# An attention and soft-mixture kernel on one core: EPS as a 33rd score column, wider products for phi and for three batches' slot averages, buffers given by a table, and the attention steps in another order

## The chip, the cores and the metric

The kernel runs on one core of a Trainium2 chip. The metric is the device time of one execution in microseconds (us), as the median of several runs. Lower is better.

## What is computed

Two stages, all in float32. Attention works on 8 batches of 8 heads, with 512 tokens and 32 state slots of 64 values each, in both directions:

```
scores = x @ state.T / 8;  a  = exp(scores - rowmax);  a  /= a.sum(-1) + 1e-09;  xread = a  @ state
scores2 = state @ x.T / 8; a2 = exp(scores2 - rowmax); a2 /= a2.sum(-1) + 1e-09; sread = a2 @ x
x = concatenate([xread, sread], axis=2), as 4608 rows of 512
```

Then a soft mixture of 8 experts with 4 slots each:

```
logits = x @ phi                                   # phi is 512 x 32
d = softmax(logits, axis 0);  slot_input = d.T @ x # 32 slots of 512
slot_out[e] = relu(slot_input[e] @ w1[e]) @ w2[e]  # w1[e] 512 x 1024, w2[e] 1024 x 512
out = softmax(logits, axis 1) @ slot_out
```

The softmaxes add EPS = 1e-09 to their sums. The weights w1 and w2 are 33.5 MB, x is 8.4 MB, and the result is 8.9 MB.

## The kernel before

**Transfers.** SyncE (SP) issues nearly all DMAs in one order: x and state first (L87 to L103), then 62 weight tiles of 512 KB and 4 of 256 KB (L112 for w2, L122 for w1), then the outputs (L789, L805). A tile pool "big" has 43 buffers of 4 KB per partition. The x tiles and the first 25 weight tiles fill it at the start. Each later weight load goes into a buffer that the kernel has finished with: two loads stand behind each batch's R step (its last use of x), one behind the later of S.7 and U.1, four 256 KB pieces go into attention's own buffers (step `load_half`), two into the "an" buffers (`load_an`), and the rest follow the w1 products, which free their weights. The framework gives each DMA one of eight semaphores in turn, and a DMA waits until the one eight places earlier has landed.

**Attention, about the first 77 us.** The order of its steps is written out by hand in the string ORDER: `X.2.1` is step X for batch 2 and head pair 1, `m2.3.0` step m2 for batch 3 and head parity 0. Engines run their own part of this list in order. The steps that matter here, for each batch b and half h:

- X, xe: TensorE (PE) turns x by 128x128 transposes; ScalarE (ACT) copies them out, scaled by 1/8 (L241). Two of batch 0 are on VectorE (DVE).
- S: scores, eight products with 32 stationary columns and 512 moving ones (L250).
- q, m1, sub, x1, l1, r1, mul, aT: token softmax. DVE turns 32x32 blocks (L263), DVE takes the maximum (L268), GpSimd (POOL) subtracts (L272), ACT takes exp (L275), DVE sums 32 scores (L279) into a two-column buffer l1s whose second column holds EPS, DVE sums those two columns (L283) and takes the reciprocal (L284), POOL multiplies (L288), DVE turns back (L293).
- m2, e2, l2: slot softmax. ACT writes its sums into l2s, again with an EPS column; DVE adds the two (L310) and inverts (L311).
- E, ee, A, ae: more PE transposes and their ACT copies (L326, L335).
- R, sr, srT, srTe: slot averages. R has 16 products per half, each with 32 stationary columns and 64 moving ones, for four groups g of 32 rows (L343). DVE scales them (L356), PE turns them (L361), ACT copies (L367).
- G, Ge: once, phi times all states: 32 products with 64 moving columns against a block-diagonal copy of phi (L206), copied by ACT (L215).
- For each pair of batches: Lx (logits), mx, mk, bm, nme (a running maximum), dx, dT, dTe, T, tt, Px, Y, which add the pair's part of slot_input into y. Ls to Ys do the same for the state rows.

The list ends with a serial stretch: the last Lx, mx.3, mk.3, bm.3, nme.3, dx.3, dT.3, dTe.3, T.3, tt.3, Px.3, Y.3, SI, SIe. SIe writes si_m, which the experts need.

**Experts and output, from about 77 us.** PE multiplies si_m by w1 (L680), turns the hidden rows (L701), and multiplies by w2 (L744), first for the left 256 columns (c = 0), then for the right. Output products (L778, L796) stand between the w2 products of c = 1; ACT and DVE copy them out (L787, L788), and SP sends them (L789).

Each kind of buffer is a rotating pool: 11 of tag "h" (2 KB), two "an", and the eight PSUM banks as 2 "sc", 3 "tr" and 3 "ms".

Of the kernel before, what the change touches and what calls it, by code (L numbers as in the profile page):

```python
# [28 lines left out]
ORDER = """
X.0.0 xe.0.0 X.0.1 xe.0.1 X.0.2 xe.0.2 X.0.3 xe.0.3 S.0 q.0.0 X.1.1 xe.1.1 X.1.2 xe.1.2 X.1.3 m2.0.0 e2.0.0  # L30
X.1.0 E.0.0 xe.1.3 m1.0.0 G.0 q.0.1 sub.0.0 m1.0.1 xe.1.0 m2.0.1 x1.0.0 l1.0.0 sub.0.1 r1.0.0 e2.0.1 l2.0 x1.0.1
X.2.1 xe.2.1 l1.0.1 Ge.0 S.1 ee.0.0 E.0.1 r1.0.1 ee.0.1 X.2.3 xe.2.3 R.0.0 q.1.0 m2.1.0 X.2.0 X.2.2 R.0.1 e2.1.0
mul.0.1 E.1.0 m2.1.1 m1.1.0 mul.0.0 q.1.1 xe.2.0 xe.2.2 e2.1.1 aT.0.1 X.3.2 sub.1.0 x1.1.0 X.3.3 aT.0.0 xe.3.3
S.2 xe.3.2 sr.0 X.3.1 m1.1.1 ee.1.0 xe.3.1 E.1.1 l1.1.0 m2.2.0 sub.1.1 x1.1.1 ee.1.1 X.3.0 q.2.0 srT.0 A.0.0
srTe.0 m2.2.1 R.1.0 q.2.1 Lx.0.0 ae.0.0 xe.3.0 R.1.1 e2.2.0 m1.2.0 l1.1.1 e2.2.1 Lx.0.1 r1.1.0 A.0.1 ae.0.1 l2.1
X.4.3 xe.4.3 m1.2.1 sr.1 r1.1.1 E.2.0 S.3 E.2.1 sub.2.0 x1.2.0 l2.2 mul.1.0 aT.1.0 q.3.1 ee.2.0 srT.1 m2.3.0
X.4.1 ee.2.1 mul.1.1 aT.1.1 X.4.0 X.4.2 Lx.1.0 m1.3.1 l1.2.0 R.2.0 Lx.1.1 xe.4.1 mx.0 srTe.1 R.2.1 A.1.0 xe.4.0
e2.3.0 m2.3.1 sub.2.1 x1.2.1 q.3.0 xe.4.2 mk.0 sr.2 l1.2.1 e2.3.1 E.3.0 ee.3.0 sub.3.1 A.1.1 ae.1.1 keep.0 bm.0
srT.2 r1.2.0 mul.2.0 S.4 nme.0 m1.3.0 R.3.0 X.5.3 dx.0 r1.2.1 mul.2.1 x1.3.1 q.4.0 l1.3.1 E.3.1 ae.1.0 xe.5.3
aT.2.0 X.5.1 aT.2.1 ee.3.1 dT.0 m1.4.0 X.5.0 m2.4.0 xe.5.1 A.2.0 dTe.0 sub.3.0 x1.3.0 srTe.2 l2.3 xe.5.0 e2.4.0  # L40
m2.4.1 q.4.1 sub.4.0 X.5.2 T.0 r1.3.1 R.3.1 Lx.2.0 m1.4.1 U.0 l1.3.0 ae.2.0 xe.5.2 tt.0 X.6.3 sr.3 mul.3.1
e2.4.1 x1.4.0 Ue.0 E.4.0 S.5 r1.3.0 A.2.1 srT.3 l1.4.0 ee.4.0 q.5.0 E.4.1 xe.6.3 sub.4.1 ae.2.1 X.6.1 x1.4.1
mul.3.0 X.6.2 Lx.2.1 R.4.0 l2.4 srTe.3 Ls.0 ee.4.1 r1.4.0 R.4.1 m2.5.1 aT.3.1 e2.5.1 Lse.0 aT.3.0 Lx.3.0 A.3.0
al.0 xe.6.2 xe.6.1 E.5.1 m2.5.0 e2.5.0 m1.5.0 sub.5.0 l1.4.1 ae.3.0 q.5.1 X.6.0 sr.4 xe.6.0 r1.4.1 mul.4.1
ee.5.1 Lr.0 msx.0 x1.5.0 Lx.3.1 Px.0 S.6 als.0 mx.1 mk.1 m1.5.1 dsx.0 lkp.0 E.5.0 A.3.1 l1.5.0 ee.5.0 sub.5.1
X.7.2 m2.6.1 R.5.0 Y.0 aT.4.1 m2.6.0 q.6.0 pv.1 X.7.3 bm.1 nme.1 ae.3.1 xe.7.2 mul.4.0 aT.4.0 X.7.0 m1.6.0
e2.6.1 r1.5.0 E.6.1 xe.7.3 e2.6.0 xe.7.0 l2.6 X.7.1 xe.7.1 R.5.1 srT.4 x1.5.1 V.0 q.6.1 l2.5 dx.1 Lu.0 m1.6.1
E.6.0 ee.6.0 sr.5 keep.1 D.0 l1.5.1 srTe.4 sub.6.1 S.7 pv.2 ee.6.1 q.7.1 mul.5.0 m2.7.1 srT.5 Ve.0 srTe.5 R.6.0
r1.5.1 mul.5.1 m2.7.0 Lx.4.0 q.7.0 R.6.1 aT.5.0 dT.1 dTe.1 Lx.4.1 A.4.1 sr.6 e2.7.1 T.1 tt.1 sub.6.0 A.4.0
e2.7.0 E.7.0 ae.4.1 x1.6.0 ee.7.0 Lus.0 m1.7.0 al.1 srT.6 E.7.1 sub.7.0 Lx.5.0 Ps.0 srTe.6 m1.7.1 aT.5.1 l1.6.0  # L50
A.5.1 sub.7.1 Ys.0 l2.7 Lu.1 r1.6.0 x1.6.1 l1.6.1 R.7.0 Lx.5.1 mx.2 mul.6.0 ee.7.1 R.7.1 sr.7 srT.7 ae.5.1
x1.7.0 r1.6.1 l1.7.0 ae.4.0 mk.2 mul.6.1 bm.2 nme.2 A.5.0 keep.2 srTe.7 Px.1 Ls.1 aT.6.0 x1.7.1 dx.2 ae.5.0 U.1
r1.7.0 mul.7.0 Lse.1 l1.7.1 dT.2 r1.7.1 mul.7.1 A.6.0 dTe.2 aT.6.1 al.2 Lx.6.0 aT.7.0 Y.1 Lr.1 msx.1 pv.3 dsx.1
lkp.1 Ue.1 Lx.6.1 Lx.7.0 T.2 ae.6.0 als.1 aT.7.1 Lx.7.1 mx.3 mk.3 A.6.1 ae.6.1 A.7.0 ae.7.0 bm.3 nme.3 dx.3 tt.2
A.7.1 Px.2 D.1 Y.2 dT.3 ae.7.1 dTe.3 V.1 Lu.2 al.3 windows keep.3 Ve.1 Lus.1 Lu.3 T.3 tt.3 Ps.1 Ys.1 load_half
load_an Wd We Px.3 spin.3 Y.3 SI SIe
"""
# [820 lines left out]
```

## Time and profile before

| what | us |
|---|---|
| median of 3 runs | 132.95 |
| lowest and highest run | 132.51, 133.6 |
| the profiled execution, whole | 132.75 |
| its span, first to last instruction | 130.9 |
| PE, DVE, ACT, POOL busy in the span | 116.0, 88.3, 76.8, 45.2 |

The profiled execution takes 1.85 us outside its span. Busy times are unions of an engine's instructions; matmuls are pipelined, so that PE's busy share overstates its load. The DMA share is the mean busy share of the core's 16 DMA engines, which can read slightly over 1.

### The profile page before, as it was taken

What the parts mean: (1) busy time and instruction counts of PE and PEld (TensorE: products, weight loads), DVE (VectorE), ACT (ScalarE), POOL (GpSimd) and SP (SyncE); (2) the same over time, 40 slices, a digit from 0 to 9 for tenths busy, and PEclk for the clock granted to TensorE, in tenths of its full rate; (3) what the DMA queues carried; (4) which work ended last, traced back from release to release, by engine and by line L of the source; (5) the groups of instructions that cost most, each with busy time, mean ns of one, the idle gap of its engine ahead of it and who ended that gap; (6) DMA issues with size and microseconds to landing.
All of it is one profiled execution on the core that took longest, in us unless ns stands there. A gap on an engine that the chain in (4) does not pass through costs nothing.

```text
span 130.9 us, 4551 instructions
## 1 busy us (share of the span) xinstructions
PE 116.0 (89%) x1854; PEld 76.2 (58%) x1854; DVE 88.3 (67%) x224; ACT 76.8 (59%) x187; POOL 45.2 (35%) x65
## 2 busy tenths in 40 slices
...
DMA  4999999999999999999999999999999999999991
GB/s 105 369 402 350 418 414 423 410 418 412 412 419 414 419 417 418 418 417 414 418 414 420 412 415 404 417 420 414 418 420 414 412 400 415 418 380 420 414 409 76
DMA packets 14852, 51.73 MB, mean 395 GB/s; under 512 B 1648, under 2 KB 1776, under 8 KB 14832
## 3 DMA queue, kind: packets, MB, share of 16 engines
...
q8 instruction: 14, 0.23, 0.6%
...
HBM read 42.53 MB, written 8.91 MB: 393 GB/s over the span
## 4 chain that ended last, share of the span: by engine, by line
DMA 57%; PE 31%; DVE 1%; issue 1%; ACT 1%; SPq 1%; DVEq 0%
DMA w<-w_in 45%; DMA x<-x_in 12%; PE so_ps L744 11%; PE h_ps L680 11%; PE o L778 6%; DVE out L788 1%; PE hT_ps L701 1%; PE sum_ps L764 1%; PE os L796 1%; ACT out L787 0%; SPq L89 0%; SPq L87 0%; PE si_ps L628 0%; ACT so_r L768 0%; DVE si_m L646 0%
## 5 line engine op out<-in xcount | busy, mean ns | idle before, releaser
L272 POOL TENSOR_TENSOR q<-q,m 128x512 f32<-128x512 f32 x16 | 16.7, 1048 | 15.4 <-DVE m L268 8.1
L241 ACT ACTIVATE xt<-xt_ps 128x512 f32<-128x512 f32 x30 | 17.9, 618 | 6.7 <-PE xt_ps L235 6.6
L288 POOL TENSOR_TENSOR q<-q,r 128x512 f32<-128x512 f32 x16 | 16.7, 1048 | 8.3 <-DVE r L284 2.7
L235 PE MATMUL xt_ps<-ident,x 128*128 128x128 f32 x112 | 16.0, 277 | 0.0
L744 PE MATMUL so_ps<-w,h_m 128*32 128x256 f32 x256 | 15.2, 381 | 0.0
L788 DVE COPY out<-o 128x512 f32<-128x512 f32 x16 | 10.3, 686 | 7.1 <-PE o L778 7.1
L680 PE MATMUL h_ps<-w,si_m 128*32 128x512 f32 x128 | 14.4, 594 | 0.4 <-DVE si_m L646 0.4
L787 ACT COPY out<-o 128x512 f32<-128x512 f32 x16 | 8.6, 590 | 8.9 <-PE o L778 8.9
L235 PEld LDWEIGHTS xt_ps<-ident,x 128*128 128x128 f32 x112 | 12.4, 141 | 2.3 <-issue 0.8
L744 PEld LDWEIGHTS so_ps<-w,h_m 128*32 128x32 f32 x256 | 7.7, 110 | 8.2 <-issue 2.3
L263 DVE STREAM_TRANSPOSE q<-sc 128x512 f32<-128x512 f32 x16 | 11.1, 695 | 1.1 <-PE sc L250 1.1
L304 ACT ACTIVATE e<-sc,nm 128x512 f32<-128x512 f32 x16 | 11.2, 706 | 0.6 <-DVE q L263 0.4
L680 PEld LDWEIGHTS h_ps<-w,si_m 128*32 128x32 f32 x128 | 9.1, 110 | 4.2 <-issue 2.3
L778 PE MATMUL o<-lt_all,so_r 32*128 32x512 f32 x64 | 10.7, 633 | 0.3
L293 DVE STREAM_TRANSPOSE aT<-q 128x512 f32<-128x512 f32 x16 | 10.8, 689 | 0.0
L279 DVE TENSOR_REDUCE l1s<-q 128x16 f32<-128x512 f32 x16 | 10.5, 656 | 0.0
L318 PE MATMUL eT_ps<-ident,e 128*128 128x128 f32 x64 | 9.9, 278 | 0.7 <-ACT e L304 0.5
L275 ACT ACTIVATE q<-q 128x512 f32<-128x512 f32 x16 | 10.5, 657 | 0.0
L268 DVE TENSOR_REDUCE m<-q 128x16 f32<-128x512 f32 x16 | 10.5, 659 | 0.0
L299 DVE TENSOR_REDUCE nm<-sc 128x1 f32<-128x512 f32 x16 | 10.5, 660 | 0.0
L318 PE MATMUL an_ps<-ident,aT 128*128 128x128 f32 x64 | 10.0, 280 | 0.2 <-DVE aT L293 0.2
L326 ACT COPY eT<-eT_ps 128x512 f32<-128x512 f32 x16 | 9.5, 608 | 0.3 <-PE eT_ps L318 0.3
...
## 6 DMA issues: line engine op xcount, KB each, us to landing
w<-w_in SPq DMA_DIRECT2D x62, 512.0 KB, 10.0
out_x<-out SPq DMA_DIRECT2D x16, 512.0 KB, 6.1
x<-x_in SPq DMA_DIRECT2D x14, 512.0 KB, 9.8
...
x_b<-x_in ACTq DMA_DIRECT2D x1, 512.0 KB, 4.6
...
```

What stands on the lines that cost most here:

```text
L235: pe.transpose(p[:, P * j : P * j + P], xg[b, g][:, j, :], ident)
L241: scaled(r[f"xt{g}"], r[f"xp{g}"], 0.125)
L263: dve.transpose(r[f"q{h}"], r[f"sp{h}"])
L272: pool.tensor_tensor(v, v, R[b][f"m1{h}"].broadcast_to([P, 16, NS]), op=ALU.subtract)
L288: pool.tensor_tensor(v, v, R[b][f"r1{h}"].broadcast_to([P, 16, NS]), op=ALU.mult)
L293: dve.transpose(r[f"aT{h}"], r[f"q{h}"])
L304: act.activation(r[f"e2{h}"], r[f"sp{h}"], AF.Exp, bias=r[f"nm2{h}"], accum_out=l2s[:, b % 2, h, 0:1])
L318: pe.transpose(p[:, j, :], r[f"{src}{h}"][:, P * j : P * j + P], ident)
L680: pe.matmul(h_ps[hf][32 * kt : 32 * kt + 32, :], si_m[kt // 2][:, 256 * (kt % 2) + 32 * e : 256 * (kt % 2) + 32 * e + 32], w1t[hf, e, kt], ...
L744: pe.matmul(so[c][32 * i : 32 * i + 32, :], h_m[hf][:, 256 * i + 32 * e : 256 * i + 32 * e + 32], w2t[c, e, 4 * hf + i], start=(hf == 0 an ...
L778: pe.matmul(o[j], so_r[hf][rows, col : col + 128], lt_all[rows, 4 * q : 4 * q + 4, :].rearrange("p b s -> p (b s)"), start=True, stop=True,)
L788: dve.tensor_copy(ot[:, 1, :], o[2 * jp + 1])
```

## The change

- The score tile q gets 33 columns for each token instead of 32. POOL writes EPS into the 33rd before `sub`, and `l1` sums 33 columns, so that L283 goes. The steps q, m1, sub, x1, mul and aT now walk over rows of 32 with a step of 33.
- e2 puts its sums straight into the tile l2; POOL adds EPS (new step `l2p`), and L310 goes.
- G takes phi itself as moving or stationary operand: 8 products with 256 moving columns and a contraction of 64 instead of 32 products with 64; Ge becomes two DVE transposes instead of an ACT copy, and the block-diagonal phi goes.
- R for batches 2, 4 and 6 (WIDE): per half 8 products with 64 stationary columns and 128 moving ones instead of 16 with 32 and 64. Half of what they write isn't used. sr is twice as wide there, and srT is two transposes.
- HOMES says by a letter which buffer each tile gets. DVE_STEPS names the copies that DVE makes instead of ACT. ORDER is a new list.
- SP's list of DMAs stays the same, in the same order; `load_half` stands earlier among the steps and `load_an` later.

The diff, cut to its core (line numbers of the new file differ):

```
 ORDER = """
-X.0.0 xe.0.0 X.0.1 xe.0.1 X.0.2 xe.0.2 X.0.3 xe.0.3 S.0 q.0.0 X.1.1 xe.1.1 X.1.2 xe.1.2 X.1.3 m2.0.0 e2.0.0
...
+X.0.0 X.0.2 xe.0.0 X.0.1 xe.0.2 X.0.3 xe.0.1 xe.0.3 X.1.1 S.0 xe.1.1 X.1.0 m2.0.1 X.1.3 xe.1.0 X.1.2 q.0.1
...
+COPIES = {"h": NH, "an": AN, "sc": 2, "tr": 3, "ms": 3}
+HOMES = {
...
+    "an": "abababbaab",
+    "sc": "abbaabababababab",
...
+DVE_STEPS = "Ve.1 ae.6.0 ae.7.1 dTe.3 lkp.1 mk.1 mk.3 xe.0.1 xe.1.1 xe.2.0"
+WIDE = (2, 4, 6,)
...
-    l1s = cp.tile([P, 4, 16, 2], F32, name="l1s")
-    l2s = cp.tile([P, 2, 2, 2], F32, name="l2s")
-    pool.memset(l1s, EPS)
-    pool.memset(l2s, EPS)
+    eps = cp.tile([P, 2, 1], F32, name="eps")
+    pool.memset(eps, EPS)
...
+        pools = {"h": wk, "an": wk, "sc": ps_s, "tr": ps_t, "ms": ps_m}
+        sizes = {"h": 16 * (NS + 1), "an": F, "sc": S, "tr": S, "ms": S}
+        def home(kind, shape, name):
+            k, n, table = made[kind], COPIES[kind], HOMES.get(kind)
+            made[kind] += 1
+            if table:
+                letter = table[k] if k < len(table) else chr(97 + (k - len(table)) % n)
+                t = pools[kind].tile([P, sizes[kind]], F32, tag=kind + letter, name=name, bufs=1)
...
+        def move(step, out, in_, scale=None):
+            if scale is None:
+                (dve.tensor_copy if step in on_dve else act.copy)(out, in_)
+            else:
+                (dve.tensor_scalar_mul if step in on_dve else act.mul)(out, in_, scale)
...
         def G(b):
-            for b in range(B):
-                for g in range(4):
+            for g in range(4):
+                for h in range(2):
+                    rows = slice(64 * h, 64 * h + 64)
                     pe.matmul(
-                        p[32 * g : 32 * g + 32, b, :],
-                        st_t(b, g),
-                        phi_bd[:, g].rearrange("p h n -> p (h n)"),
+                        gp[h][32 * g : 32 * g + 32].rearrange("p (q i) n -> p q i n", i=2),
+                        phi_sb[rows, g, :],
+                        stT_sb[rows, :, g % 2, g // 2, :, :],
...
         def Ge(b):
-            act.copy(G_sb, R[0]["gp"].rearrange("p b (h n) -> p b h n", h=2))
+            for h in range(2):
+                dve.transpose(G_sb[:, :, h, :], R[0]["gp"][h])
...
         def q(b, h):
-            r[f"q{h}"] = half(f"q{b}_{h}")
-            dve.transpose(r[f"q{h}"], r[f"sp{h}"])
+            t = home("h", [P, 16, NS + 1], f"q{b}_{h}")
+            r[f"qv{h}"] = t[:, :, 0:NS]
+            dve.transpose(r[f"qv{h}"], r[f"sp{h}"].rearrange("p (k n) -> p k n", n=NS))
...
         def sub(b, h):
+            pool.memset(R[b][f"q{h}"][:, :, NS : NS + 1], EPS)
             pool.tensor_tensor(v, v, R[b][f"m1{h}"].broadcast_to([P, 16, NS]), op=ALU.subtract)
...
         def l1(b, h):
-            i = 2 * (b % 2) + h
-            dve.tensor_reduce(out=l1s[:, i, :, 0:1], in_=R[b][f"qv{h}"], axis=AX.X, op=ALU.add)
+            R[b][f"r1{h}"] = t = sm.tile([P, 16, 1], F32, tag=f"r1{h}", name=f"r1_{b}_{h}")
+            dve.tensor_reduce(out=t, in_=R[b][f"q{h}"], axis=AX.X, op=ALU.add)
         def r1(b, h):
-            dve.tensor_reduce(out=t, in_=l1s[:, 2 * (b % 2) + h], axis=AX.X, op=ALU.add)
             dve.reciprocal(t, t)
...
+        def l2p(b):
+            pool.tensor_tensor(R[b]["l2"], R[b]["l2"], eps, op=ALU.add)
         def l2(b):
-            dve.tensor_reduce(out=t, in_=l2s[:, b % 2], axis=AX.X, op=ALU.add)
             dve.reciprocal(t, t)
...
         def R_(b, h):
+            w = 2 if b in WIDE else 1
             for j in range(NJ):
-                for g in range(4):
+                for g in range(0, 4, w):
+                    v = xg[b, g][:, j] if w == 1 else pairs[b, g // 2][:, :, j]
+                    rows = slice(32 * g, 32 * (g + w))
                     pe.matmul(
-                        r["srp"][32 * g : 32 * g + 32, h, :],
-                        r[f"eT{h}"][:, j, 32 * g : 32 * g + 32],
-                        xg[b, g][:, j, D * h : D * h + D],
+                        r["srp"][rows, h],
+                        r[f"eT{h}"][:, j, rows],
+                        v[..., D * h : D * h + D],
...
         def srT(b):
-            pe.transpose(r["srTp"], r["sr"].rearrange("p h d -> p (h d)"), ident)
+            for i in range(2 if b in WIDE else 1):
+                pe.transpose(r["srTp"][:, P * i : P * i + P], r["sr"][:, i].rearrange("p h d -> p (h d)"), ident)
```

On PE the wide products show in batch 2. This is its R step for the half 0 and what stands around it, before (sr_ps2 is the PSUM tile of the averages, eT2_0 the turned exponentials, x2_0 and x2_1 the two tiles of x; x2 at a row's end means two equal ones in a row):

```order
L375 MATMUL lt_0_531<-aT1_0_623,G_sb_120 32x128 x4
L343 MATMUL sr_ps2_660<-x2_0_77,eT2_0_627 32x64 x2
L343 MATMUL sr_ps2_660<-x2_1_79,eT2_0_627 32x64 x2
L343 MATMUL sr_ps2_660<-x2_0_77,eT2_0_627 32x64 x2
L343 MATMUL sr_ps2_660<-x2_1_79,eT2_0_627 32x64 x2
L343 MATMUL sr_ps2_660<-x2_0_77,eT2_0_627 32x64 x2
L343 MATMUL sr_ps2_660<-x2_1_79,eT2_0_627 32x64 x2
L343 MATMUL sr_ps2_660<-x2_0_77,eT2_0_627 32x64 x2
L343 MATMUL sr_ps2_660<-x2_1_79,eT2_0_627 32x64 x2
L375 MATMUL lt_0_531<-aT1_1_641,G_sb_120 32x128 x4
```

And after, at the same step:

```order
L354 MATMUL an_ps1_1_618<-ident_103,aT1_1_595 128x128 x4
L382 MATMUL sr_ps2_627<-x2_0_77,eT2_0_597 64x128
L382 MATMUL sr_ps2_627<-x2_1_79,eT2_0_597 64x128
L382 MATMUL sr_ps2_627<-x2_0_77,eT2_0_597 64x128
L382 MATMUL sr_ps2_627<-x2_1_79,eT2_0_597 64x128
L382 MATMUL sr_ps2_627<-x2_0_77,eT2_0_597 64x128
L382 MATMUL sr_ps2_627<-x2_1_79,eT2_0_597 64x128
L382 MATMUL sr_ps2_627<-x2_0_77,eT2_0_597 64x128
L382 MATMUL sr_ps2_627<-x2_1_79,eT2_0_597 64x128
L354 MATMUL an_ps1_0_643<-ident_103,aT1_0_625 128x128 x4
```

Sixteen products of 32x64 became eight of 64x128, and transposes for batch 1 (an_ps1) stand around them where the logits (lt_0) stood. On DVE, the token softmax of batch 2 before (q2 holds its scores, r1_2 the sums' reciprocals, m1 and nm2 maxima):

```order
L356 TENSOR_TENSOR sr_2_725<-sr_ps2_660,l2_2_619 128x128
L279 TENSOR_REDUCE l1s_115<-q2_1_529 128x16
L283 TENSOR_REDUCE r1_2_0_750<-l1s_115 128x16
L284 RECIPROCAL r1_2_0_750<-r1_2_0_750 128x16
L455 TENSOR_REDUCE nm_all_123<-bm_ps0_746 128x1
L268 TENSOR_REDUCE m1_3_0_765<-q3_0_719 128x16
L283 TENSOR_REDUCE r1_2_1_792<-l1s_115 128x16
L284 RECIPROCAL r1_2_1_792<-r1_2_1_792 128x16
```

And after:

```order
L347 RECIPROCAL l2_2_469<-l2_2_469 128x2
L314 TENSOR_REDUCE r1_2_0_663<-q2_0_446 128x16
L439 TENSOR_REDUCE mx_0_684<-lt_0_483 128x1
L302 TENSOR_REDUCE m1_3_1_686<-q3_1_648 128x16
L297 STREAM_TRANSPOSE q3_0_694<-sc3_0_569 128x16x32
L318 RECIPROCAL r1_2_0_663<-r1_2_0_663 128x16
L314 TENSOR_REDUCE r1_2_1_711<-q2_1_481 128x16
L302 TENSOR_REDUCE m1_3_0_727<-q3_0_694 128x16
L397 TENSOR_TENSOR sr_2_730<-sr_ps2_627,l2_2_469 128x2x2x64
```

The short second sum (L283) is gone, other work stands between a sum and its reciprocal, and sr_2 is twice as wide.

## Rows read from the trace of the kernel before

**Rows 1.** The page's slices, 40 of 3.27 us each: DMA busy share in tenths, and GB/s.

```profile
DMA  4999999999999999999999999999999999999991
GB/s 105 369 402 350 418 414 423 410 418 412 412 419 414 419 417 418 418 417 414 418 414 420 412 415 404 417 420 414 418 420 414 412 400 415 418 380 420 414 409 76
```

**Rows 2.** The DMA queue's own waits (SP): line waited for, us in total, times, longest; and the first line of the DMA issues: times, KB each, median us from issue to landing.

```profile
SPq L112 <- DMA w<-w_in: 27.6, 34, 1.6
SPq L122 <- DMA w<-w_in: 20.8, 23, 1.3
...
w<-w_in SPq DMA_DIRECT2D x62, 512.0 KB, 10.0
```

**Rows 3.** Stretches of the span: start:end, length, busy us of PE, PEld (weight loads), DVE, ACT, POOL with instruction counts, granted PE clock, DMA share, GB/s.

```profile
12.00:104.00 92.00, 89.79 (x1646) 63.88 (x1650) 72.49 (x195) 63.49 (x163) 42.79 (x53) 1.00 1.03 416
104.00:108.00 4.00, 4.00 (x60) 1.74 (x56) 1.95 (x4) 1.48 (x3) 0.00 (x0) 1.00 0.98 399
108.00:116.00 8.00, 7.87 (x85) 3.30 (x78) 4.29 (x9) 3.80 (x9) 0.00 (x0) 1.00 1.02 414
116.00:118.00 2.00, 1.88 (x14) 1.23 (x14) 1.98 (x4) 1.68 (x4) 0.00 (x0) 1.00 0.89 362
118.00:131.00 13.00, 2.75 (x16) 1.08 (x12) 2.80 (x5) 2.15 (x4) 0.00 (x0) 0.76 0.81 328
```

**Rows 4.** SP's timeline of issues: start, us until the last one's end, line, transfer, count.

```profile
58.67 40.51 SPq L112 DMA_DIRECT2D w<-w_in  x34
104.13 8.87 SPq L789 DMA_DIRECT2D out_x<-out  x8
113.88 0.33 SPq L805 DMA_DIRECT2D out_s<-out_s  x1
116.05 2.76 SPq L789 DMA_DIRECT2D out_x<-out  x4
118.91 1.10 SPq L805 DMA_DIRECT2D out_s<-out_s  x1
120.11 4.19 SPq L789 DMA_DIRECT2D out_x<-out  x4
```

**Rows 5.** The chain that ended last, in order of time: start, us, what.

```profile
77.36 0.20 DVE si_m L646
77.60 9.06 PE h_ps L680 x80
...
120.79 0.69 DVE out L788
```

**Rows 6.** The same columns as in rows 3, for the body of attention and its end.

```profile
14.00:68.00 54.00, 52.61 (x1094) 39.95 (x1095) 52.98 (x141) 52.07 (x133) 30.73 (x35) 1.00 1.03 416
68.00:77.60 9.60, 8.85 (x172) 6.21 (x168) 5.16 (x19) 5.46 (x18) 3.12 (x10) 1.00 1.02 416
```

**Rows 7.** Groups of instructions up to 78 us, shapes apart: line, engine, operation, out<-in, shapes, count | busy us, mean ns | idle before.

```profile
L241 ACT ACTIVATE xt<-xt_ps 128x512 f32<-128x512 f32 x30 | 17.9, 618 | 6.7 <-PE xt_ps L235 6.6
L263 DVE STREAM_TRANSPOSE q<-sc 128x512 f32<-128x512 f32 x16 | 11.1, 695 | 1.1 <-PE sc L250 1.1
L279 DVE TENSOR_REDUCE l1s<-q 128x16 f32<-128x512 f32 x16 | 10.5, 656 | 0.0
L335 ACT COPY an<-an_ps 128x512 f32<-128x512 f32 x16 | 9.7, 607 | 0.0
L326 ACT COPY eT<-eT_ps 128x512 f32<-128x512 f32 x16 | 9.5, 608 | 0.3 <-PE eT_ps L318 0.3
L283 DVE TENSOR_REDUCE r<-l1s 128x16 f32<-128x32 f32 x16 | 2.7, 170 | 0.1
L356 DVE TENSOR_TENSOR sr<-sr_ps,l 128x128 f32<-128x128 f32 x8 | 2.1, 262 | 0.0
L391 DVE TENSOR_REDUCE mx<-lt 128x1 f32<-128x256 f32 x4 | 1.7, 416 | 0.5 <-PE lt L375 0.5
L241 DVE TENSOR_SCALAR xt<-xt_ps 128x512 f32<-128x512 f32 x2 | 1.4, 692 | 4.9 <-PE xt_ps L235 4.9
L503 DVE STREAM_TRANSPOSE tt<-t_ps 128x128 f32<-128x128 f32 x4 | 1.2, 306 | 1.9 <-PE t_ps L492 1.9
L310 DVE TENSOR_REDUCE l<-l2s 128x2 f32<-128x4 f32 x8 | 0.9, 114 | 0.0
L215 ACT COPY G_sb<-g_ps 128x512 f32<-128x512 f32 x1 | 0.6, 584 | 0.0
L441 POOL TENSOR_TENSOR l_row<-l_row,lx 128x1 f32<-128x1 f32 x3 | 0.6, 190 | 0.2
```

**Rows 8.** PE's timeline: start, us from the first start to the last end, line, shapes, count of records (each product but a transpose has two).

```profile
12.66 0.32 PE L206 MATMUL g_ps<-phi_bd,x_a 128*32 128x64 f32 x8
...
13.69 0.66 PE L235 MATMUL xt_ps<-ident,x 128*128 128x128 f32 x4
14.28 1.17 PE L250 MATMUL sc<-xt,stT_sb 64*32 64x512 f32 x16
...
63.09 0.65 PE L343 MATMUL sr_ps<-x,eT 128*32 128x64 f32 x32
63.56 0.40 PE L375 MATMUL lt<-aT,G_sb 128*32 128x128 f32 x8
63.77 0.63 PE L343 MATMUL sr_ps<-x,eT 128*32 128x64 f32 x32
```

More of the change, by code (lines that the diff above doesn't have):

```diff
@@ L26 @@
 NH = 11
+AN = 2
 ORDER = """
-X.0.0 xe.0.0 X.0.1 xe.0.1 X.0.2 xe.0.2 X.0.3 xe.0.3 S.0 q.0.0 X.1.1 xe.1.1 X.1.2 xe.1.2 X.1.3 m2.0.0 e2.0.0
[L31 to L54, printed above, removed]
@@ L55 @@
-A.7.1 Px.2 D.1 Y.2 dT.3 ae.7.1 dTe.3 V.1 Lu.2 al.3 windows keep.3 Ve.1 Lus.1 Lu.3 T.3 tt.3 Ps.1 Ys.1 load_half
-load_an Wd We Px.3 spin.3 Y.3 SI SIe
-"""
+X.0.0 X.0.2 xe.0.0 X.0.1 xe.0.2 X.0.3 xe.0.1 xe.0.3 X.1.1 S.0 xe.1.1 X.1.0 m2.0.1 X.1.3 xe.1.0 X.1.2 q.0.1
+xe.1.3 q.0.0 e2.0.1 m2.0.0 X.2.0 xe.1.2 m1.0.0 E.0.1 e2.0.0 X.2.1 xe.2.0 sub.0.0 ee.0.1 S.1 m1.0.1 xe.2.1 l2p.0
+X.2.3 sub.0.1 x1.0.0 l2.0 m2.1.0 E.0.0 xe.2.3 m2.1.1 X.2.2 ee.0.0 q.1.1 X.3.0 xe.2.2 R.0.0 q.1.0 e2.1.1 R.0.1
+m1.1.1 G.0 e2.1.0 l1.0.0 S.2 sub.1.1 xe.3.0 sr.0 Ge.0 x1.0.1 r1.0.0 X.3.3 m1.1.0 x1.1.1 mul.0.0 E.1.1 m2.2.0
@@ new lines @@
+xe.3.3 E.1.0 q.2.0 ee.1.1 sub.1.0 U.0 ee.1.0 aT.0.0 srT.0 X.3.1 e2.2.0 l1.0.1 A.0.0 l2p.1 Ue.0 q.2.1 Lx.0.0
+R.1.0 x1.1.0 r1.0.1 l1.1.1 X.3.2 ae.0.0 mul.0.1 R.1.1 xe.3.1 m2.2.1 E.2.0 xe.3.2 l1.1.0 X.4.1 e2.2.1 r1.1.1
+X.4.3 l2.1 aT.0.1 srTe.0 mul.1.1 S.3 r1.1.0 sr.1 xe.4.3 m1.2.0 l2p.2 mul.1.0 srT.1 X.4.0 aT.1.1 ee.2.0 Lx.0.1
+xe.4.1 m2.3.0 sub.2.0 E.2.1 xe.4.0 m1.2.1 A.1.1 ee.2.1 aT.1.0 R.2.0 ae.1.1 sub.2.1 m2.3.1 x1.2.0 A.1.0 q.3.1
+X.4.2 e2.3.0 l2.2 Lx.1.0 l1.2.0 Lx.1.1 x1.2.1 R.2.1 xe.4.2 mx.0 m1.3.1 ae.1.0 E.3.0 q.3.0 e2.3.1 A.0.1 X.5.1
```

136 lines of the change are left out of this document (85 added, 51 removed).

## Prediction

> **What bounds the kernel now.** I read the slices of the page first. From the third slice to the last but one the 16 DMA engines are busy nine tenths or more, at about 415 GB/s [rows 1]. The stretch from 12 to 104 us as a whole has a DMA share of 1.03 and 416 GB/s [rows 3]. So the transfers look like the bound, and the next question is whether they ever wait for the engines.
>
> The queue's own waits say no for the weights. SP waits 27.6 + 20.8 us on the landing of earlier weight loads, 57 times, never over 1.6 us, and a load lands 10.0 us after its issue [rows 2]. That is the wait for one of eight places: the queue is full, and up to the last weight load at 99.2 us [rows 4] only the memory sets its pace. Nothing that attention does in that time can make it faster.
>
> Then come the outputs, which do wait for the engines. I count what is still queued when the first output is issued at 104.13 us [rows 4]. After 104 us the stretches move 4 x 399 + 8 x 414 + 2 x 362 + 13 x 328 = 9.90 MB [rows 3]. Sixteen outputs of 524 KB and two of 262 KB are 8.91 MB. The difference, 0.99 MB, is weights, worth 2.4 us at 416 GB/s. At 116 us I count again: 2 x 362 + 13 x 328 = 4.99 MB move, and the issues from 116.05 on (eight of 524 KB, one of 262 KB [rows 4]) are 4.46 MB. So only 0.53 MB, or 1.3 us, are queued, and the share sinks to 0.89 [rows 3]. The queue is nearly empty there. At the end it is full again: the last copy ends at 121.5 us [rows 5], with the queue still sending until near 129.
>
> The chain behind the outputs is PE's. si_m comes at 77.36, the w1 products start at 77.60, and from there the chain of waits stays nearly all on PE up to the last copy at 120.79 [rows 5]; PE is busy 7.87 of 8 us even among the outputs [rows 3]. So the kernel is balanced in an uneven way. If attention ends earlier, the outputs come earlier, but the queue can only fill its holes: 4 x (1 - 399/416) + 8 x (1 - 414/416) + 2 x (1 - 362/416) = 0.16 + 0.04 + 0.26 = 0.46 us. If attention ends later, the holes grow, nearly one us for each us.
>
> **What attention costs now.** Between 14 and 68 us DVE is busy 52.98 of 54, ACT 52.07, POOL 30.73 [rows 6]. PE's 52.61 says little, as its matmuls are pipelined. So DVE sets the pace, with ACT close behind. From 68 to 77.6 us DVE and ACT are busy 5.16 and 5.46 of 9.6: a serial end.
>
> **The change on DVE.** It removes L283, 16 x 170 ns = 2.72 us, and L310, 8 x 114 = 0.91 [rows 7]. It adds:
> - one more xt copy (three instead of two): 0.69 [rows 7].
> - Ge as two transposes of 128x256. None of that size is in the trace; 128x128 takes 306 ns and 128x512 takes 695 [rows 7]. Between them I take 436, so 0.87; bounds 0.6 to 1.4.
> - sr of twice the width for three batches: 262 ns for 128 columns; the nearest 128x256 operation takes 416 [rows 7]. 3 x 154 = 0.46; bounds 0 to 0.8.
> - 16 more columns in each l1: at 656 ns for 512 [rows 7] that is 20 ns, 16 times: 0.33.
>
> Sum: -2.72 - 0.91 + 0.69 + 0.87 + 0.46 + 0.33 = -1.3 us. The step of 33 I price at nothing: ACT writes its strided an copy in 607 ns and its plain eT copy in 608 [rows 7]. The trace has no such step on DVE or POOL; if each of 64 DVE passes cost 5% of 0.66 us, the gain would turn into +0.8. The other side is no gain, because a pass of 512 elements can't need less than it does contiguously.
>
> **On ACT:** the G_sb copy goes (0.58) and one xt copy net (0.62) [rows 7]: -1.2 us before the end stretch. Both pacing engines lose about the same, so I let the body of attention end 1.2 us earlier, at the same idle time. The new order itself may win or lose waits; with 1.0 us idle on DVE and 1.9 on ACT in that body [rows 6] it can't win over 1 us, and may lose 2.
>
> **In the end stretch** DVE takes three copies of 128x512, two smaller ones and mk.3. At the 0.69 us that a 128x512 copy takes there [rows 7], that is about 3 us, beside 4.4 us in which DVE idles [rows 6]. They stand among nme.3, dTe.3 and tt.3, which the serial end waits for: bounds -0.5 to +0.7, taken as 0.
>
> **On POOL:** 16 small memsets and 8 l2p, at most the 190 ns of a 128x1 addition [rows 7] each: 4.6 us beside 23 us of idle time [rows 6]. POOL takes its work in order, so an l2p that waits for e2's sums holds back the sub and mul behind it, and with them x1 and l1. The idle time hides it where the order leaves room; without that, 8 x 0.2 = 1.6 us.
>
> **On PE:** per half, R has 32 records of 64 columns from 63.09 to 63.56, 0.47 us; Lx has 8 of 128 columns in the next 0.21 [rows 8]. That is 2048 columns at 4.4 and 1024 at 4.9 a ns: the pace goes by columns, not by records. The wide R has as many columns in all, but on stationary blocks twice as wide, of which half as many fit beside each other: 0.84 to 0.94 us, if that halves the pace; 0.23 if records set it. I take +0.4 x 6 = +2.4 us, and three more transposes, +0.4. G took 12.66 to 13.69, 1.03 us; as half of a score step (14.28 on, 1.1 us) it takes 0.55 [rows 8]. In all +2.3, bounds -2 to +3. I leave it outside the sum, as DVE and ACT pace the body; it is the second rival's price.
>
> The Trainium skill, "TensorEngine Tiling (Array Packing)", Tiling Modes, says the same in general: 32 stationary columns give four tiles that run at once, 64 give two. By that rule the wide products cost PE time instead of saving it, and the rows of R agree with the four. The same page, Instruction Overhead, puts some 60 cycles on each matmul, by which fewer and wider ones would be a gain; by it the sum here would stay as it is, since PE isn't in it.
>
> **Transfers:** bytes, order and queue stay the same. Loads whose buffers come free later have 10 us of queued work ahead of them [rows 2], so a shift of a few us isn't seen.
>
> **Sum.** The profiled execution took 132.75 us: 130.9 of span and 1.85 around it. si_m comes 1.2 us earlier, and all outputs with it. The queue fills holes worth 0.46; I take 0.4, since some of the dip after 104 us may be reads and writes in the same queue. 132.75 - 0.4 = **132.35 us**, 0.5% under the shown median of 132.95.
>
> **Rivals.**
> 1. Attention's gain arrives whole at the end: 132.75 - 1.2 = 131.5, or 130.8 with 0.7 more from the order. For it: from 77 us on the chain of waits is PE's. Against it: the DMA share of 1.03 at 416 GB/s over 92 us [rows 3]. It needs a queue that could go faster. The Trainium skill, "DMA: Bandwidth & Descriptors", Specifications, puts the fabric's ceiling at 435 GB/s; by that figure there would be 4% of room, but the rows show none used with every engine busy. 0.08.
> 2. Slower: PE becomes the bound of attention through the wide R products. Place: batches 2, 4 and 6, where sr, srT and the transposes behind R wait. Price: if the +2.3 us aren't hidden, si_m comes 2.3 - 1.2 = 1.1 us late, or 2.3 when DVE's gain is lost to the waiting. The holes after 104 us grow by as much: 133.85 to 135.05. It decides from the first tenths of a us, since the queue is at 1.3 us at 116 us and already dips. For it: the pace by columns. Against it: DVE and ACT leave under 2 us idle in the body [rows 6], and their share of the work is what shrinks. 0.16.
> 3. The change does nothing that can be seen: DVE's saving is lost to waits in the new order, si_m stays at 77.4, and the time at 132.75. It lies within the likeliest's range. 0.16.
>
> **How the numbers follow.** The likeliest has 0.6, with an own range of 131.9 to 132.9. About 1% (1.3 us) is what a measurement of this kernel can tell from no change. Faster by over that needs rival 1: 0.09 with the likeliest's tail. Slower by over that is most of rival 2: 0.14. The rest, 0.77, is within 1%. The range for 8 in 10 takes in the likeliest, the third rival and the near half of the second: 131.6 to 134.0.
>
> **What would show it.** Right: si_m written between 75.5 and 77 us; the DMA share at 1.0 and over 400 GB/s in every slice between 104 and 122 us; the last w2 load again issued near 99 us, whatever attention does; DVE without its 24 short sums; and a span shorter by much less than si_m's shift. Wrong: weight loads that end earlier than 98 us (the queue had room), si_m after 78.5 us with a dip at 104 or 116 us that is wider by the same amount, or q, m1, l1 and aT instructions longer by over 5% from the step of 33.

## The result, and the profile after

The changed kernel takes 134.94 us (median of 4 runs, 134.69 to 135.06); the kernel before, beside it, 133.03. The ratio is 1.014, with a 95% interval of 1.0095 to 1.0184. The prediction was 132.35, in a range that ended at 134.0, so the kernel lies above the range and on the side that had 0.14. The profiled execution took 134.69 us with a span of 132.9.

The slices of the page come first, as in [rows 1].

```profile
DMA  3999999999999999999999999999999999999994
GB/s 111 341 371 403 416 407 411 412 407 413 393 408 407 412 406 412 407 406 407 407 416 401 411 399 398 406 407 409 401 411 412 407 365 386 409 396 382 404 409 184
```

The DMA engines are as busy as before, but where most slices of [rows 1] have 414 to 420 GB/s, most now have 406 to 412. The stretches of [rows 3] and [rows 6] say it in one number (same columns: stretch, length, busy us of PE, PEld, DVE, ACT, POOL, granted PE clock, DMA share, GB/s).

```profile
12.00:104.00 92.00, 90.76 (x1477) 65.66 (x1474) 74.97 (x181) 61.47 (x153) 45.37 (x76) 1.00 1.03 407
104.00:108.00 4.00, 4.00 (x56) 1.93 (x52) 1.58 (x3) 1.34 (x3) 0.00 (x0) 1.00 0.93 371
108.00:116.00 8.00, 8.00 (x106) 3.26 (x100) 3.87 (x6) 3.37 (x7) 0.00 (x0) 1.00 0.99 399
116.00:118.00 2.00, 1.87 (x16) 1.03 (x16) 1.01 (x3) 0.75 (x3) 0.00 (x0) 1.00 1.02 414
118.00:131.00 13.00, 5.72 (x32) 2.62 (x26) 5.49 (x9) 4.57 (x9) 0.00 (x0) 0.83 0.99 397
14.00:68.00 54.00, 53.90 (x954) 40.38 (x953) 51.35 (x115) 49.85 (x122) 32.67 (x55) 1.00 1.03 408
68.00:77.60 9.60, 9.35 (x188) 7.70 (x190) 8.23 (x25) 6.55 (x22) 5.54 (x13) 1.00 1.03 407
```

A DMA share of 1.03 with 407 GB/s, where it was 1.03 with 416: the same time of the engines moves 2.2% fewer bytes. In the records of the packets, those of 4096 bytes between 12 and 104 us take 163.2 ns on average, and 160.0 before. The whole program moves 51.71 MB. By an estimate that takes these rates for all of it, that is 127.1 us at 407 GB/s and 124.3 at 416: 2.7 us, more than the time that was lost.

SP's timeline of issues, beside [rows 4]:

```profile
59.73 41.36 SPq L125 DMA_DIRECT2D w<-w_in  x34
107.22 8.87 SPq L837 DMA_DIRECT2D out_x<-out  x8
116.97 0.33 SPq L853 DMA_DIRECT2D out_s<-out_s  x1
119.14 2.92 SPq L837 DMA_DIRECT2D out_x<-out  x4
122.16 1.12 SPq L853 DMA_DIRECT2D out_s<-out_s  x1
123.38 4.47 SPq L837 DMA_DIRECT2D out_x<-out  x4
```

The weights' issues end at 101.1 instead of 99.2 us, and the outputs start 3.1 us later. The chain that ended last, beside [rows 5], shows where those 3.1 us arise:

```profile
80.45 0.20 DVE si_m L694
80.69 9.06 PE h_ps L728 x80
...
123.88 0.69 DVE out L836
```

So two things went the wrong way: the transfers are slower all through, and si_m comes 3.1 us later, not 1.2 earlier. Either could explain 2 us. The single instructions, beside [rows 7], are as they were priced:

```profile
L307 POOL TENSOR_TENSOR q<-q,m 128x512 f32<-128x512 f32 x16 | 16.8, 1051 | 17.2 <-DVE m L302 17.2
L327 DVE STREAM_TRANSPOSE aT<-q 128x512 f32<-128x512 f32 x16 | 11.0, 692 | 0.5 <-PE sc L283 0.3 <-PE eT_ps L354 0.2
L314 DVE TENSOR_REDUCE r<-q 128x16 f32<-128x528 f32 x16 | 10.8, 682 | 0.0
L302 DVE TENSOR_REDUCE m<-q 128x16 f32<-128x512 f32 x16 | 10.6, 660 | 0.0
L306 POOL MEMSET q<- 128x16 f32 x16 | 2.0, 128 | 1.1 <-PE sr_ps L382 1.1
L343 POOL TENSOR_TENSOR l<-l,eps 128x2 f32<-128x2 f32 x8 | 1.6, 197 | 1.1 <-ACT e L340 1.1
L397 DVE TENSOR_TENSOR sr<-sr_ps,l 128x256 f32<-128x256 f32 x3 | 1.2, 394 | 0.0
L249 DVE STREAM_TRANSPOSE G_sb<-g_ps 128x256 f32<-128x256 f32 x2 | 0.8, 424 | 0.0
```

In the kernel before, aT and POOL's subtraction were:

```profile
L293 DVE STREAM_TRANSPOSE aT<-q 128x512 f32<-128x512 f32 x16 | 10.8, 689 | 0.0
L272 POOL TENSOR_TENSOR q<-q,m 128x512 f32<-128x512 f32 x16 | 16.7, 1048 | 15.4 <-DVE m L268 8.1 <-ACT eT L326 4.3 <-ACT xt L241 2.6
```

PE's timeline around a wide product of R, and the chain around a narrow one, beside [rows 8]; in the first the pitch from the wide block to the next is 31.40 - 30.38 = 1.02 us:

```profile
30.38 1.09 PE L382 MATMUL sr_ps<-x,eT 128*64 128x128 f32 x16
31.40 0.66 PE L354 MATMUL an_ps<-ident,aT 128*128 128x128 f32 x4
```

```profile
67.08 0.58 PE sr_ps L382 x32
67.67 1.02 PE an_ps L354 x8
```

A wide half takes 1.02 us, a narrow one 0.58 (0.47 in [rows 8]): about the halved pace that the prediction assumed.

### The profile page after: what moved, and what is told of

It reads as the page before. It is cut to its first block, busy times and chain, and to the rows that moved or that the text cites. A ratio compares the mean times of both kernels' runs of the same rounds, so it can differ in the third digit from the quotient of the medians.

```text
span 132.9 us, 4266 instructions
## 1 busy us (share of the span) xinstructions
PE 120.6 (91%) x1713; PEld 80.8 (61%) x1713; DVE 89.9 (68%) x210; ACT 74.7 (56%) x178; POOL 46.6 (35%) x85
## 2 busy tenths in 40 slices
DMA packets 14851, 51.71 MB, mean 389 GB/s; under 512 B 1648, under 2 KB 1776, under 8 KB 14832
## 4 chain that ended last, share of the span: by engine, by line
PE 82%; DVE 4%; DMA 4%; ACT 2%; issue 1%; DVEq 0%
PE xt_ps L269 12%; PE so_ps L792 11%; PE h_ps L728 11%; PE sr_ps L382 9%; PE sc L283 7%; PE eT_ps L354 6%; PE o L826 6%; PE an_ps L354 5%; DMA x_a<-x_in 4%; PE lt L423 3%; PE t_ps L540 2%; DVE aT L327 1%; PE px_ps L574 1%; PE srT_ps L403 1%; DVE out L836 1%
## 5 line engine op out<-in xcount | busy, mean ns | idle before, releaser
L307 POOL TENSOR_TENSOR q<-q,m 128x512 f32<-128x512 f32 x16 | 16.8, 1051 | 17.2 <-DVE m L302 17.2
L217 ACT ACTIVATE xt<-xt_ps 128x512 f32<-128x512 f32 x29 | 17.3, 609 | 9.5 <-PE xt_ps L269 9.1
L269 PE MATMUL xt_ps<-ident,x 128*128 128x128 f32 x112 | 17.0, 284 | 0.0
L269 PEld LDWEIGHTS xt_ps<-ident,x 128*128 128x128 f32 x112 | 12.9, 145 | 4.5 <-issue 1.4
L382 PE MATMUL sr_ps<-x,eT 128*32 128x64 f32 (+1 forms) x352 | 11.3, 237 | 0.0
L314 DVE TENSOR_REDUCE r<-q 128x16 f32<-128x528 f32 x16 | 10.8, 682 | 0.0
L310 ACT ACTIVATE q<-q 128x512 f32<-128x512 f32 x16 | 10.1, 650 | 0.0
L382 PEld LDWEIGHTS sr_ps<-x,eT 128*32 128x32 f32 (+1 forms) x352 | 9.1, 117 | 1.6 <-issue 0.9
```

Of the source, the lines that this page charges most:

```text
L217: (dve.tensor_scalar_mul if step in on_dve else act.mul)(out, in_, scale)
L269: pe.transpose(p[:, P * j : P * j + P], xg[b, g][:, j, :], ident)
L382: pe.matmul(r["srp"][rows, h], r[f"eT{h}"][:, j, rows], v[..., D * h : D * h + D], start=(j == 0), stop=(j == NJ - 1),)
```

## The experiments

Theory A: late outputs alone set the time. Theory B: something in the changed kernel slows every transfer. They were parted first, by a control and by shifting si_m without touching the rest.

**The control** is the kernel before, unchanged.

> The kernel before, unchanged, run as a candidate on the same chip as the next three, for its transfer rate. Theory A (late outputs: the wide R products hold PE, attention ends 3.1 us late, the outputs with it) says nothing on the rate. Theory B (slower transfers: 407 GB/s instead of 416 between 12 and 104 us set the later end) comes in two forms: if the memory or the chip of that run did it, this run shows about 407 GB/s and a time near 134 us; if the changed kernel does it, this run shows 416 GB/s, si_m at 77.4 us and 133.0 us.

132.76 us, ratio 0.9999 (0.9974 to 1.0025).

```profile
12.00:104.00 92.00, 89.21 (x1634) 63.66 (x1638) 71.98 (x193) 63.06 (x161) 42.79 (x53) 1.00 1.03 415
```

415 GB/s here too, so 407 belongs to the changed kernel and not to a chip. si_m came at 78.05 where the first profile has 77.36 (DVE's timeline):

```profile
78.05 0.48 DVE L646 TENSOR_TENSOR si_m<-si_ps,rl 128x32 f32<-128x32 f32 x4 [0.49 <-PE si_ps L628]
```

A difference of 0.7 us in si_m between two runs of one program means nothing.

**Narrow products in all batches, in the changed kernel.**

```diff
-WIDE = (2, 4, 6,)
+WIDE = ()
```

> The changed kernel with WIDE = (): batches 2, 4 and 6 go back to 32x64 products, all else as in the changed kernel. Theory A: R takes 0.47 to 0.55 us a half again, si_m comes near 77.5 us (between 76.5 and 78), the outputs start near 104.3, and the time is 132.6 to 133.4 us, 1.2 to 1.7% less than the changed kernel. Theory B: the rate between 12 and 104 us stays at 407 GB/s and the time at 134.3 us or more, whatever si_m does.

134.78 us, ratio 1.0147 (1.0116 to 1.0178). si_m comes 1.6 us earlier (78.86) and nothing is gained.

```profile
78.86 0.48 DVE L694 TENSOR_TENSOR si_m<-si_ps,rl 128x32 f32<-128x32 f32 x4 [0.49 <-PE si_ps L676]
12.00:104.00 92.00, 88.60 (x1578) 63.49 (x1582) 73.31 (x179) 59.91 (x152) 45.32 (x76) 1.00 1.03 407
104.00:108.00 4.00, 4.00 (x56) 1.49 (x52) 1.48 (x3) 1.30 (x3) 0.00 (x0) 1.00 1.01 405
```

Still 407 GB/s, and no dip left at 104 us: the queue is never short of work and the time is that of the transfers. Theory A falls for this kernel.

**The kernel before, with si_m late** (28 more products that only pass time ahead of it).

```diff
-Px.3 spin.3 Y.3 SI SIe
+Px.3 spin.31 Y.3 SI SIe
```

> The kernel before with 28 more PE transposes in the step spin ahead of SI, at 0.11 us each: si_m comes 3.0 us late, and nothing else of attention or of the transfers ahead of it changes. Theory A: outputs start 3.0 us later (107.1), a DMA dip stands near 119 us as in the changed kernel, and the time rises by 1.3 to 2.0 us, to 134.3 to 135.0. Theory B: the queue hides most of it; the time rises by less than 0.6 us, to 133.0 to 133.6.

135.35 us, ratio 1.0196 (1.0166 to 1.0225), si_m at 80.02.

```profile
80.02 0.49 DVE L646 TENSOR_TENSOR si_m<-si_ps,rl 128x32 f32<-128x32 f32 x4 [3.24 <-PE si_ps L628]
12.00:104.00 92.00, 90.00 (x1641) 65.80 (x1642) 71.38 (x192) 62.43 (x159) 42.63 (x53) 1.00 1.03 416
104.00:108.00 4.00, 4.00 (x56) 1.78 (x58) 1.58 (x3) 1.34 (x3) 0.00 (x0) 1.00 0.68 275
```

Lateness alone leaves 416 GB/s and makes a deep hole at 104 us (275 GB/s). The changed kernel has its lateness in the same place with a shallow one (371). So lateness can cost 2.5 us, but the picture of it is another.

**Wide products in batches 1 to 7, in the changed kernel**, one run.

```diff
-WIDE = (2, 4, 6,)
+WIDE = (1, 2, 3, 4, 5, 6, 7)
```

> The changed kernel with WIDE = (1, 2, 3, 4, 5, 6, 7): four more batches with wide R products. Theory A: 8 halves more at 0.55 us and 4 transposes at 0.11 hold PE 4.8 us longer; si_m comes 3.5 to 5 us later than in the changed kernel (84 to 85.5 us), and the time rises by nearly as much, to 138 to 139.7 us. Theory B, or PE not the bound of attention: si_m under 82.5 us and the time under 136.5.

138.29 us, si_m at 84.51.

```profile
84.51 0.48 DVE L694 TENSOR_TENSOR si_m<-si_ps,rl 128x32 f32<-128x32 f32 x4 [0.49 <-PE si_ps L676]
```

Eight wide halves more, at 1.02 - 0.58 = 0.44 us, are 3.5 us, and four more transposes at 0.11 us 0.4; si_m moved by 4.1. PE's pace does reach si_m, whole.

What slows the transfers? Bytes, order and queue of the DMAs are the same, so I looked at where their buffers lie. Pools are laid one behind the other in SBUF, the constants first, then the pool of inputs, weights and outputs. The change takes 704 bytes a partition out of the constants (l1s 512, l2s 32, three mc 160) and puts 32 in (eps). That pool began at 11264 = 44 x 256 and now begins at 10592 = 41 x 256 + 96; its places are 4096 bytes apart, so every transfer into or out of it, which is nearly all of the large ones, now starts 96 bytes past a multiple of 256. Theory C: that offset sets the rate. Rival D: the changed kernel's own traffic in SBUF does.

**The changed kernel with the pool back on a multiple of 256** (10752).

```diff
-    eps = cp.tile([P, 2, 1], F32, name="eps")
+    eps = cp.tile([P, 42, 1], F32, name="eps")[:, 0:2]
...
-            Z["rl"] = sm.tile([P, NS], F32, tag="rl", name="rl", bufs=1)
+            Z["rl"] = sm.tile([P, NS], F32, tag="D", name="rl")
```

> The changed kernel with 160 bytes more in its constants (a longer tile for EPS), so that the buffers of inputs, weights and outputs begin at a multiple of 256 bytes in each partition again, as in the kernel before (there 11264; in the changed kernel 10592, which is 96 over a multiple of 256; here 10752); rl takes a buffer of D to make room; the wide products stay. Theory C (the start of the buffers sets the transfer rate): 4096-byte packets go back from 163.2 to 160 ns, 415 to 416 GB/s over 12 to 104 us; si_m stays late (79.5 to 81), so dips come at 104 to 108 and 118 to 120 us as in the kernel before with its window 2.7 us late, and the time hardly gains: 134.2 to 135.7 us. Rival D (the changed kernel's own SBUF traffic of PE, DVE and ACT slows the transfers): packets stay at 163 ns, 407 GB/s, 134.7 to 135.0 us.

132.99 us, ratio 1.0019 (0.9974 to 1.0064), packets of 160.6 ns, si_m at 79.32.

```profile
79.32 0.48 DVE L694 TENSOR_TENSOR si_m<-si_ps,rl 128x32 f32<-128x32 f32 x4 [0.49 <-PE si_ps L676]
12.00:104.00 92.00, 90.63 (x1481) 65.59 (x1481) 74.06 (x180) 60.70 (x152) 45.30 (x76) 1.00 1.03 415
104.00:108.00 4.00, 4.00 (x52) 1.56 (x48) 1.29 (x2) 1.07 (x2) 0.00 (x0) 1.00 0.85 346
```

The rate is back, and with it the whole loss. Theory C's own time, 134.2 to 135.7, was a miss: I had taken the late si_m to cost as much as in the run with 28 more products, and it cost almost nothing.

**The same with narrow products.**

> The same, and in addition no batch has wide products. Theory C with two limits of which the later counts: rate 415 to 416 GB/s, si_m near 78.8, the time 133.3 to 134.2 us, 0.8 us or so under the changed kernel with narrow products alone (134.78) because that one's transfers were the limit. Rival D: 407 GB/s, 134.7 us.

132.92 us, ratio 1.0028 (0.9962 to 1.0093), si_m at 78.16. The time is under the forecast's lower end, and no different from the wide one's.

```profile
78.16 0.48 DVE L694 TENSOR_TENSOR si_m<-si_ps,rl 128x32 f32<-128x32 f32 x4 [0.49 <-PE si_ps L676]
12.00:104.00 92.00, 89.31 (x1582) 63.51 (x1582) 73.47 (x180) 60.05 (x153) 45.31 (x76) 1.00 1.03 416
14.00:68.00 54.00, 52.48 (x1083) 39.03 (x1083) 51.07 (x121) 50.07 (x125) 33.72 (x57) 1.00 1.03 416
```

**The kernel before, 96 bytes further on**, nothing else. This is the counter-test: the offset without any of the change.

```diff
-    mask = cp.tile([P, 4], F32, name="mask")
+    mask = cp.tile([P, 28], F32, name="mask")[:, 0:4]
```

> The kernel before with 96 bytes more in its constants (a longer tile for mask), nothing else: the buffers of the pool big begin 96 bytes over a multiple of 256, as in the changed kernel. Theory C: packets 163.2 ns, 407 GB/s over 12 to 104 us, si_m where it was (77.4 to 78.1), the time 134.2 to 135.0 us, so this alone makes the kernel as slow as the change did. Rival D: 160 ns, 416 GB/s, 132.8 us.

134.71 us, ratio 1.0154 (1.011 to 1.0197), packets of 163.1 ns.

```profile
12.00:104.00 92.00, 88.81 (x1630) 63.82 (x1631) 72.78 (x194) 63.86 (x163) 43.07 (x53) 1.00 1.03 407
104.00:108.00 4.00, 4.00 (x52) 1.51 (x52) 1.36 (x3) 1.19 (x3) 0.00 (x0) 1.00 1.02 408
```

24 unused floats in a constant make the kernel before as slow as the whole change made it. Rival D falls. One part of the forecast was a miss: si_m comes at 78.97, not at 77.4 to 78.1. The other shifted versions below have it at 78.1 to 78.7, so slower transfers may hold attention back a little; against the control's 78.05 that isn't clear of noise.

**Other offsets of the kernel before:** 224 bytes (60 floats in mask, rl in a buffer of D), 64 (20 floats) and 128 (36 floats, rl in D).

> The kernel before with 224 bytes more in its constants (and rl in a buffer of D to make room): the buffers begin 224 bytes over a multiple of 256. If the loss is the bytes of a first 256-byte piece that are moved and not used (224 in 4096, 135 pieces of 32 bytes for 128, where 96 gives 131), packets take 160 x 135/128 = 168.8 ns, 394 GB/s, and the time is 137.5 to 139.5 us. If each start off a multiple of 256 costs one and the same (a packet in 17 pieces for 16), packets take 163.2 ns and the time is 134.2 to 135.0 us.

> The kernel before with 64 bytes more in its constants, so that the buffers begin 64 bytes over a multiple of 256 (and on a multiple of 64). If every start off a multiple of 256 costs the same, as 96 and 224 did: packets 163.2 ns, 406 to 408 GB/s, 134.5 to 135.0 us. If only starts off a multiple of 64 cost it (96 and 224 are both 32 over one): 160.0 ns, 416 GB/s, 132.7 us.

> The kernel before with 128 bytes more in its constants (and rl in a buffer of D to make room), so that the buffers begin 128 bytes over a multiple of 256. If only multiples of 256 are free of loss: 163.2 ns, 406 to 408 GB/s, 134.5 to 135.0 us. If a multiple of 128 or 64 is enough: 160.0 ns, 416 GB/s, 132.7 us.

134.94 us for 224 (ratio 1.0134 to 1.0248), 134.43 for 64 (1.0095 to 1.0168) and 134.58 for 128 (1.0091 to 1.0183); packets of 163.4, 163.3 and 163.1 ns. The stretch from 12 to 104 us, one run each, in that order:

```profile
12.00:104.00 92.00, 89.45 (x1630) 63.81 (x1630) 72.08 (x193) 63.21 (x161) 42.85 (x53) 1.00 1.03 406
```

```profile
12.00:104.00 92.00, 89.02 (x1629) 63.72 (x1631) 72.67 (x194) 63.66 (x163) 43.09 (x53) 1.00 1.03 406
```

```profile
12.00:104.00 92.00, 88.71 (x1630) 63.81 (x1630) 72.10 (x193) 63.11 (x162) 43.06 (x54) 1.00 1.03 407
```

All four offsets cost the same 2% of the rate, whether 64 or 224, and 1.3 to 1.9% of the time. The forecast of 168.8 ns for 224 was a miss; its other branch held.

**A multiple of 256 that is none of 512** (10496), by laying five small constants of the changed kernel into two tiles; narrow products.

```diff
-    mask = cp.tile([P, 4], F32, name="mask")
+    both = cp.tile([P, 6], F32, name="both")
+    mask = both[:, 0:4]
...
-    eps = cp.tile([P, 2, 1], F32, name="eps")
+    eps = both[:, 4:6].rearrange("p (n o) -> p n o", o=1)
...
-    nm_all = cp.tile([P, B + 2], F32, name="nm_all")
-    al_all = cp.tile([P, B + 2], F32, name="al_all")
-    l_row = cp.tile([P, 1], F32, name="l_row")
+    alls = cp.tile([P, 2 * B + 5], F32, name="alls")
+    nm_all = alls[:, 0 : B + 2]
+    al_all = alls[:, B + 2 : 2 * B + 4]
+    l_row = alls[:, 2 * B + 4 : 2 * B + 5]
```

> The changed kernel with narrow products, its five small constants (mask and EPS; nm_all, al_all and l_row) laid together in two tiles, which takes 96 bytes out: the buffers begin at 10496, a multiple of 256 but not of 512 (those of the kernel before at 11264 and of the aligned variants at 10752, multiples of 512). If a multiple of 256 is what counts: packets 160.0 ns, 415 to 416 GB/s, 132.5 to 133.0 us. If 512 is needed: 163.2 ns, 406 to 408 GB/s, 134.4 to 134.9 us.

132.89 us, ratio 0.9997 (0.9966 to 1.0027), packets of 160.0 ns, si_m at 78.99.

```profile
78.99 0.48 DVE L696 TENSOR_TENSOR si_m<-si_ps,rl 128x32 f32<-128x32 f32 x4 [0.50 <-PE si_ps L678]
12.00:104.00 92.00, 88.47 (x1578) 63.29 (x1582) 73.71 (x180) 60.27 (x153) 45.38 (x76) 1.00 1.03 416
```

A multiple of 256 is enough.

**Earlier first scores.** In the changed kernel PE waits for batch 1's transfer (X.1.1) ahead of batch 0's scores (S.0). On top of narrow products and the pool at 10752:

```diff
-xe.0.3 X.1.1 S.0 xe.1.1 X.1.0 m2.0.1 X.1.3
+xe.0.3 S.0 m2.0.1 X.1.1 xe.1.1 X.1.0 X.1.3
```

> The changed kernel with narrow products and buffers on a multiple of 256 bytes, and in its table of steps S.0 (the first scores) and m2.0.1 moved ahead of X.1.1, which waits for batch 1's transfer (PE was without work for 1.56 us there in the same kernel without the move, and the scores began at 9.25 us, in the kernel before at 7.74). Theory: the scores begin at 7.8 us, the attention runs up to 1.5 us earlier, si_m starts at 76.7 to 77.6 (78.16 without the move), the 0.4 us in which the queue is short of work at 104 to 107 us goes, and the time is 132.2 to 132.9 us, at or a little under the kernel before. Rival: the later steps wait for transfers of x anyway, si_m stays at 78.0 to 78.4, 132.9 us.

132.84 us, ratio 1.0003 (0.998 to 1.0025); si_m at 78.24, as without the move. DVE's timeline:

```profile
9.77 0.69 DVE L333 TENSOR_REDUCE nm<-sc 128x1 f32<-128x512 f32 x1 [1.49 <-PE sc L283]
10.38 0.68 DVE L217 TENSOR_SCALAR xt<-xt_ps 128x512 f32<-128x512 f32 x1
10.97 1.30 DVE L297 STREAM_TRANSPOSE q<-sc 128x512 f32<-128x512 f32 x2
```

The scores did start 1.3 us earlier (7.92 for 9.25), but DVE's copy of batch 1 still stands between and q starts at 10.97, as it did (11.05). The edit didn't reach what it was to move, so it shows only that S.0's place by itself is worth nothing. No version tried beats the kernel before.

## Why the prediction was wrong

1. **"Transfers: bytes, order and queue stay the same"** is the step that failed. The sentence is true and its conclusion isn't: where the buffers start is a fourth property, the change moved it by 672 bytes, and no view of the trace shows an address. The diff did show it: each tile taken from or put into the constants moves everything behind it. The size of the loss follows from the prediction's own first part: if only the memory sets the pace for 92 us, 2% of the rate is near 2 us. Both halves are shown: the change without the offset is as fast as the kernel before (1.0019, 1.0028, 0.9997), and the offset without the change costs as much (1.0154, and 1.0132 to 1.0191 at the other offsets).

2. **Where the loss begins.** Pools at 10496, 10752 and 11264, all multiples of 256, lose nothing; at 64, 96, 128 and 224 bytes past a multiple the packets take 163.1 to 163.4 ns for 160.0, about 2% more at all four. The Trainium skill, "DMA: Bandwidth & Descriptors", How a descriptor splits into AXI transactions, says that a transaction must start on a 256-byte boundary, and that a transfer that starts off it fetches bytes which it doesn't use but pays for, in beats of 32 bytes. The boundary agrees with the runs, though the page tells it of bytes that are read, and here it is the place written to that moved. The size doesn't agree: an estimate by its beats for 4096 bytes is 130/128, 131/128, 132/128 and 135/128, 1.6 to 5.5% more.

3. **The balance** held in part. While the transfers run at 407 GB/s, a si_m at 78.86 or at 80.45 us makes no difference (134.78 and 134.94). At 416 GB/s, 2.0 us of lateness against the control cost 2.5 us, as "nearly one us for each us" has it; but 1.3 us (79.32) cost 0.3 (132.99 for 132.67), within the noise, and 0.9 us (78.99) nothing (132.89 for 132.93). What lets the first us go free isn't settled: in the profile of 79.32 the holes between 104 and 121 us are 1.1 us larger than the control's (bytes short of the run's own rate), while the thin end of the last transfers, from 126 us on, is 0.7 us shorter.

4. **DVE and ACT.** The prices were right: 24 short sums gone, l1 at 682 ns for 656, Ge at 424 ns for the 436 taken, the wide sr at 394, the small POOL steps 3.6 us for "at most 4.6", and the step of 33 costs nothing (aT 692 for 689, POOL 1051 for 1048). What failed is "at the same idle time". With narrow products and aligned buffers DVE works 51.07 us between 14 and 68 us where it worked 52.98 [rows 6], and idles 2.9 us where it idled 1.0. si_m comes at 78.16, and at 78.24 and 78.99 in the two other runs with narrow products and aligned buffers, against 77.36 and 78.05: the saving went into the new order's waits, as rival 3 had it. Without the offset that rival would have been the result.

5. **PE.** The wide products cost 6 x 0.44 = 2.6 us for the 2.4 taken, and rival 2's mechanism exists: eight wide halves more moved si_m by 4.1 us. What the six moved is less sure: 1.6 us without alignment (80.45 for 78.86) and 0.3 to 1.2 with it (79.32 for 78.16, 78.24 and 78.99), where runs without wide products differ by 0.8 among themselves. It isn't what made the kernel slower; the wide and narrow variants take the same time in both pairs.

6. **What was to show it.** The prediction watched for weight loads that end early (before 98 us, which would mean room in the queue). They ended late, at 101.1, which no rival had a place for: none had a slower rate of the transfers. Half of its sign for rival 2 came: si_m was written after 78.5 us, but the dips among the outputs didn't grow by the 3.1 us that si_m was late: between 104 and 121 us the bytes short of each run's own rate are worth 0.8 us, and 0.45 before.
